# Taking arithmetic off GpSimd in a fused attention and two-stage MoE kernel: low parts by VectorE, or by a negated cast on ScalarE and an adding transfer

## The chip, the cores and the metric

One core of a Trainium2 chip runs the whole kernel. Its engines are TensorE (PE in the profile, with its weight loads shown apart as PEld), VectorE (DVE), ScalarE (ACT), GpSimd (POOL) and SyncE (SP). Each works through its own instruction list in order and waits at semaphores. Transfers (DMAs) are issued from a queue of SyncE or of GpSimd and run beside the engines. The metric is the device time of one launch in microseconds, the median over several runs.

## The reference

The input is 2 x 4096 tokens of 192 features, seen as 8192 tokens. A causal window of 7 tokens is mixed with softmax weights (8 heads of 24 features), then two wide layers follow:

```python
w = softmax(weight_gen)                       # over the 7 taps
out[b, s, h] = sum_k w[b, s, h, k] * x_pad[b, s + k, h]
gate = 1 / (1 + exp(-(x @ w_gate)))           # 192 -> 1536
x = (gate * (x @ w_val)) @ w_out              # 1536 -> 192
h = x @ w_in                                  # 192 -> 2048
P = a0 + a1*h + a2*h**2 + a3*h**3
Q = 1 + abs(b0)*abs(h) + abs(b1)*h**2
out = (P / (Q + 1e-6)) @ w_out2               # 2048 -> 192
```

The weights arrive as 64-bit floats, and everything is computed to fp32 accuracy. TensorE's fp32r format holds fewer bits, so each operand of the first three products is split into a high part (the value rounded to fp32r) and a low part (the value minus its high part), and a product is made of several matmuls.

## The kernel before, in words

The tokens are cut into 17 blocks: 15 of 4 x 128 tokens and 2 of 2 x 128. A block passes through a chain of small steps. Each step is a Python function whose name begins with `do_`; it issues a few instructions and puts the next step into a waiting list with `then(...)`. The string `ORDER` (3947 words, one for each step) says which step is issued next. This fixes the instruction order on every engine, since each engine works in the order of issue. There is no other scheduler.

The steps that matter here:

- Weight preparation: `K` loads a piece of the weights (SyncE's queue), `Ka` takes magnitudes (ACT), `Kd` packs 64-bit words into fp32 (DVE; function `pack`, lines 187 to 193), `Kh` casts the high part (ACT), and `kl` makes the low part by subtracting (POOL, line 373). `Kc` places the tails (transfers of SyncE). There are 25 pieces, 17 of which have low parts, with two subtractions each.
- Attention: `B` multiplies a shifted window by its weights (DVE, line 283). The seven products are summed by `J` (an adding transfer from GpSimd's queue, line 430) or by `j` (an addition on DVE, line 428). `Z` and `T1` transpose the block on PE; `C1` and `L1` split it into high and low.
- First layer, a unit of 128 of the 1536 columns at a time (192 units in all): `g` and `v` are five matmuls each into PSUM (`in_proj`), `S` is the sigmoid (ACT, line 490), `M` multiplies by the value (DVE, line 502), `G` casts the high part `gh` (ACT, line 508). Then `L` (on DVE) or `l` (on POOL) makes the low part `gl = g1 - gh` (line 514), and `O` is five matmuls into the accumulator.
- Second layer, 256 units: `H` is five matmuls, `A` three activations (ACT), `V` and `W` the polynomial (DVE, lines 605 and 610). Then, on pairs of units, `Q` adds the parts of the denominator by an adding transfer from GpSimd's queue (line 621), or `q` does so on DVE (line 619). `R` and `U` are activations (lines 626 and 631) that give a first reciprocal, `T` (DVE, line 614) or `t` (POOL, lines 643 and 644) together with `Y` and `D` (both DVE, line 614) finish the quotient, and `P` is the matmuls of the output product (line 669).
- `F` copies the finished block out of PSUM (ACT, line 678) and stores it.

A step with two names, such as `do_L_l`, has one body and two engines: the first name passes VectorE as `eng`, the second GpSimd. In `do_J_j` and `do_Q_q` it is the other way about: `J` and `Q` issue the transfer from GpSimd's queue, `j` and `q` add on DVE.

Buffers are rings. `bufs` tells how many tiles a name has; a tile is used again once all readers of its former content are done. PSUM has one bank each for `g` and `v`, two for `h`, and two accumulators.

Of the kernel before, what the change touches and what calls it, by code (L numbers as in the profile page):

```python
# [45 lines left out]
G v E S O E1 J l M E2 O Kd kl C2 B G g j Ka L2 Ka v Kd G H l S g M O Kd K Kc J Ka B S v g j Ka l K G O A V Z S W T1 M
C1 G kl l v X g Ka kl L1 H O A M S Kd G v l H g S O V Kc W M A v Q Kd g K R S B V Kd l G W B H M B L H O v A g Kd U O
M Q S V W G Kc L v G A Y Na M g S H O A g V W l O V T v S G R M g G W U S J H J L H v M O l D G O v M g A v S B t E l
V M G g S O A W g E1 V v Q S Q j l W H P P R Y G U A H B L R O T M v Y D U M O V g G S W A P L G H v V W P M g Ka l Kd
H S A E2 g j V v B W S A Q O V g M W G R U T Q D H L O v C2 Y H P L2 R G M P S A J v U O t A D V g l W Q H B V W O S Y  # L50
J A X P M g G H v G Y P V l S W A D M L O Z T H V g v G A W V O P S Nb W M D T1 Q Nc R v P R l M C1 B L1 P H G g H U v
A B V W l U j S Y H A A O V W g Q P T B H V W G S M g O D T Y l v R B H P O A S M G E g D Q G L P V v S E1 O g J A U l
B P R M W Q T Y G V H W U v O R M A v E2 L D V W H G L A O P Y O S H V M t Q g U G W F L v H A P V S W g T H M A S J D
P Y V J q P R A U R v W T C2 H P V M W A D O V g W H G L2 l Q B S A Y v H O U G M l g P A V P S D R V P W W T B H U T
J A V j W g v Y O H P G S M A l H v V Z X G D g M Q O A l V S W v g G W R M T1 q O U Y v P C1 l G R S D P Y O L1 H H T
A M g V A B W l G P V Q H L S P W B U g Y D A Q V S R J v W U H A R O T M H Y V W O A G v M P g U H V W D Na T S H P E
B Y g l G Q J v P A S V A E1 W g M S O v L G T Q R H P D U F L R g E2 O B A O P V W M v H D V W M S G A H g L v T Y S
P D G g V P W U C2 A l T Nb Y V H W L2 B P A M D J Q H O v M S V g Q W A O G L v S H J O V R M P G A B P J W V H U Q B
L W v G R g U A S Y T L O H V M P Y A v R D O j Nc P G g M W H V S G g W A L Z v V U O W M S Q R G v L Y P T T1 X C1 P
M L1 T O D H g v S H B A P V B W g l B A G H U S V O l M v g O Y D M A Q V S j P W R T P H Q E v G j B P U W R g A l  # L60
E1 M G O V H v D j P S B l Y A M B g G P U W T l S T D H A O G V v g W M H E2 Y J C2 Q S L A v g V M F O O W S V Q W H
R G G H B P A V U g L O A W l P L2 v H S V W D T M P g Y H q R v A G A M U D V O P P W Y V l R H G W S O v T H Q U g A
V X A D W M P J S G H J v g S V q Z L O W Na M A T G V l W R g P H P O H A Y D V W L U v Q A R V P M v W S T1 O P C1 Y
T L1 D g G H U S A M H G g A v S T L Q O V Y W B l D V W R O M E H B P A V q E1 W U G Y R v H g E2 M T R P P j U S H l
v A g G Y V W P O H A M V D C2 v W L S G T g U A M O B Q H S L Y P O V R W B A P G v H Nb V J W g T F M D l J S A B V
H D O Q g v P A S M G U G V v P L2 l g Q W H R M B W U A H l O R O G T V Y T W P L U A V P Q v Y S H M D J A g J O v S
g R W V Y M H B S A W P H Q T v V W P g H G D A S G A L D J Q P V W U P H g R V A W M X L v O Y P Nc M Z G R V U S W v
l T1 T C1 P Y O G L1 O M B H B j A l B U V H g D S O Q v G g A l S M O P R g U W Y v V G T E W H M v P H A L S E1 V W
D H T O g D M G A G V Y W P S g Q A T v S l D g l J R Q P U M H A V W V E2 R Y P B H v T U O A P M O V W B G W F H D l
S v Y C2 G M A Q H J g L2 V S O R A l W v G P P U T H M B O V J W D g S v Y H G g A A P Q B T V W S P H L R g V J P q  # L70
l W U A H M V D R O U v S A Y T T W O P Y V W P G Q H A g M V D S v R l G H O M W v H L P G U O g A A L M D V V J W v
Z X S W T1 B C1 G L1 P P Q H R H Na g A L P M O A O S T Y U B Q v V G l g Nb J D W S M V T H v M W O A B G g B v V E S
Q E1 G R l U M H P Y A R E2 O W V D P W H l A Q V Y g v H T S M U G O P W g G l T S A Y H D C2 Nc v M R l J O V W A G
g S P O P Q H j A l v g V B F S W H M V v W M G P L2 U P l A O Y g V R D P S W B T H D v J O J A H M g G U v V W A V Y
L W Q H S Q R g S U M P O H g T v B D A V A G Q T P W P G Y V L H W S P R A M j L H R P A U V W D V v H A O Z M O G g
q G V T W v W l Y T1 C1 L P S P L1 H g M U H S D A g A T O X B v G V Y S W R O U Q M g V G W B H R U v P J D T Y A P S
l V W H O l M A T V H A G v g S M P q B Q P J g W E E1 D v V l Y M R H O W U A P O H P D G l R S A F V W g G B T H V Y
A v S W U M H P Q E2 V D J L A V B v O W B C2 O G P q l M g W R P S H L2 Y G l H v g T M v D A O U V S A G M j g L S W
v P Y T H P V O g R D q P W A U H R O G M Y V S A B W v V L g U J H W H Q M S J T D g G A A O V G W V P H Y S X T W Q
v R L P A P U V Z M W O G l v T1 Na Y O M C1 L1 P R H H g v l T U B A S D O G V P g A Q W B D M l V H S W g G A Y S V  # L80
W v P T l H O J q R A E V R g H D M A P P V W q P U W G R T H H l v S Y M g v A S P B V A M g E1 O F U G E2 W J D U S
Y T l D v B H O g A O M V W v V C2 Nb H W P G H G q S L A g T Y P l M V R J L2 W A O v B P H B P G V W H U M O D J Q T
S A P A V G W L l g V H Q R v A S W Y M U Q B O H D v Nc g S P M G O V T g A Y S X G V W v j P W L H R U M A Y P H v l
D A V O R O J W M q V g W G T Z v P T1 R S l U O M C1 P G L1 D H A L g H S V A W Q v g T G V O S U H Y W R A M l O v g
E Y T E1 G M H q V D P P B S v G B l M O U W J P g v A R l V Y S H O E2 M g B A D U V Q v W T G P S W H C2 g J l A G O
V M S W H A P Q g R B v L2 G S L Y l P O T F M H D g A U v V D P G P W S H Y V W M j H g R v P A B A V T Q W L M V W U
O G O J R G B H S L P A Y U H v g D J l A V W O M Q B T S P H G j V A v W O V Y P D Q M H R W A V T D g G l P R H P U
v L W A V W S Y M T H O g Q A S P Z V v X W T1 D G C1 P P M L1 H g Na U O P B H B A S L Y Q V R v U W g J A R G T S D
H O M v T P l B g J G A V Q O W H L V Y E U B P M G v E1 S W O T A L g H M V S W D v O A G H L q M P V g R v Y R W U T
D O H P S M A A G V W V L g Y G v S H O E2 J B W F U l j C2 M A L2 P g V S H g A v Q G P B D S Q W H R V W H M O A A G  # L90
l g V B W V l v W H P M Y P S O Nb T U D Y v R T H A V g W A V Q P D G W P M U O H P G R A Y L X T H l J V S W Nc v M
A O g P S D H O j G Z V v W A l U M Q V g W G v T S q O T1 P R C1 U L1 M P H R Y T U l g v O D S g M H A V G G W B S Y
Q H A B P g S j v B l V g M A L D V W v O S G g H Y P E l R E1 M T v A P O M U G Q R W V W S Y D H A P H J B V U W v O
g H G l S P E2 B T O A V g W Y M A P Q v l S T C2 F V G D R W D H Q J P A H U M A l R V O T W v M g B O U Y P Y V L2 W
J S H v G L G g S J A B T P g H M S X V j W P Q R A O D U g v Z H L V G W P D M Q T P A H V O A L v P W O G V W Y H M
# [666 lines left out]
```

## Time and profile before

| what | value |
|---|---|
| median of 3 runs | 1437.95 us (1434.44 to 1438.52) |
| the profiled execution's own time | 1437.92 us |
| its span, first to last instruction | 1436.1 us |
| PE busy | 1337.7 us, 93% |
| DVE busy | 1313.3 us, 91% |
| ACT busy | 1176.3 us, 82% |
| POOL busy | 422.0 us, 29% |
| chain that ended last | PE 50%, DVE 25%, ACT 11%, issue 7%, DMA 4% |
| transfers from GpSimd's queue | 85.67 MB, 32.4% of the 16 DMA engines' span |
| mean granted TensorE clock | 0.993 |

"Busy" is the time in which at least one instruction of the engine runs. DVE and ACT start an instruction shortly before the one in front has ended, so the sum of single durations is a little larger than busy time. The chain is followed back from the last instruction, at each step to what released it. POOL's busy time holds its arithmetic and the issuing of its transfers.

### The profile page before, as it was taken

The numbers are of one execution on the slowest core, as the hardware profiler recorded it, in microseconds if no ns is written. First come the engines' busy times: TensorE is split into PE (matmuls) and PEld (weight loads), VectorE is DVE, ScalarE is ACT, GpSimd is POOL, SyncE is SP. The second block draws the span as 40 slices with busy tenths as digits, with TensorE's granted clock in tenths as the row PEclk, the third lists the DMA queues.
The fourth block names the chain that finished last, engine by engine and source line by source line (L and its number), as shares of the span: only waits on it lengthen the run. The fifth ranks groups of instructions, "written<-read, shape, count | busy, mean of one in ns | idle before, by whom it ended". The sixth has DMA issues, their size and how long they took to land.

```text
span 1436.1 us, 18208 instructions
## 1 busy us (share of the span) xinstructions
PE 1337.7 (93%) x6602; PEld 1144.8 (80%) x6602; DVE 1313.3 (91%) x1568; ACT 1176.3 (82%) x1761; POOL 422.0 (29%) x368
## 2 busy tenths in 40 slices
PE   1778999999999999999999999999999999989987
PEld 0556787888878788888888888888888888878886
DVE  7999898999888999889999999899999999999997
ACT  4555878989878898889988898888978889878985
POOL 3654442322132122323212222222123231452220
PEclk9999999999999999999999999999999999999999
DMA  9765343434434245444514324354425342313433
GB/s 247 185 171 132 74 97 67 85 84 99 103 68 98 45 90 107 97 107 81 120 29 85 89 59 94 67 126 78 97 41 103 78 76 68 71 32 74 85 74 67
DMA packets 48946, 130.94 MB, mean 91 GB/s; under 512 B 6236, under 2 KB 15834, under 8 KB 48856
## 3 DMA queue, kind: packets, MB, share of 16 engines
q0 software_dynamic: 27504, 85.67, 32.4%
q1 hardware_dynamic: 21064, 44.11, 10.1%
q8 instruction: 52, 0.85, 0.2%
q14 instruction: 38, 0.31, 0.1%
q10 hardware_dynamic: 288, 0.00, 0.0%
HBM read 31.51 MB, written 6.29 MB: 26 GB/s over the span
## 4 chain that ended last, share of the span: by engine, by line
PE 50%; DVE 25%; ACT 11%; issue 7%; DMA 4%; POOL 1%; SPq 1%; DVEq 0%; ACTq 0%; POOLq 0%
PE acc L669 12%; DVE v L614 6%; DVE v L605 3%; DVE v L610 3%; PE h L295 3%; DVE g L502 3%; PE h L296 2%; PE h L299 2%; PE h L297 2%; PE h L298 2%; DVE q L614 2%; DVE pr L283 2%; PE pv L295 2%; ACT v L596 2%; ACT r L598 2%
## 5 line engine op out<-in xcount | busy, mean ns | idle before, releaser
L669 PE MATMUL acc<-wo,v 128*128 128x192 f32 x2048 | 367.6, 326 | 5.8 <-DVE v L614 5.8
L669 PEld LDWEIGHTS acc<-wo,v 128*128 128x128 f32 x2048 | 340.7, 189 | 21.5 <-DVE v L614 7.1
L514 POOL TENSOR_TENSOR gl<-g,gh 128x512 fp32r<-128x512 f32 x119 | 185.2, 1559 | 428.7 <-ACT gh L508 395.3
L605 DVE TENSOR_TENSOR v<-v,h 128x512 f32<-128x512 f32 x256 | 174.3, 681 | 67.6 <-ACT r L598 66.8
L596 ACT ACTIVATE v<-h,co 128x512 f32<-128x512 f32 x256 | 176.5, 689 | 69.6 <-PE h L299 61.7
L621 POOL DMA_DIRECT2D q<-r x105 | 94.3, 898 | 408.0 <-ACT r L598 371.2
L610 DVE SCALAR_TENSOR_TENSOR v<-v,co,h 128x512 f32<-128x512 f32 x256 | 189.7, 743 | 3.8
L614 DVE SCALAR_TENSOR_TENSOR v<-v,co,r 128x1024 f32<-128x1024 f32 x128 | 185.9, 1453 | 0.4 <-ACT r L631 0.3
L614 DVE SCALAR_TENSOR_TENSOR v<-q,v 128x1024 f32<-128x1024 f32 x128 | 169.8, 1327 | 0.6
L598 ACT ACTIVATE r<-h 128x512 f32<-128x512 f32 x256 | 155.6, 608 | 8.5 <-DVE q L614 5.4
L490 ACT ACTIVATE sg<-pg 128x512 f32<-128x512 f32 x192 | 116.0, 604 | 55.6 <-PE pg L299 48.9
L614 DVE SCALAR_TENSOR_TENSOR q<-q,r 128x1024 f32<-128x1024 f32 x120 | 159.0, 1328 | 0.4 <-ACT r L631 0.4
L597 ACT ACTIVATE q<-h 128x512 f32<-128x512 f32 x256 | 153.4, 599 | 5.7 <-DVE v L614 5.7
L626 ACT ACTIVATE r<-q,co 128x1024 f32<-128x1024 f32 x128 | 147.7, 1155 | 10.4 <-DMA q<-r 5.3
L502 DVE TENSOR_TENSOR g<-sg,pv 128x512 f32<-128x512 f32 x192 | 130.6, 680 | 24.0 <-PE pv L299 18.4
L295 PE MATMUL h<-X2h,W0h 128*128 128x512 f32 (+1 forms) x272 | 118.0, 434 | 23.5 <-DVE v L610 20.2
L508 ACT CAST gh<-g 128x512 fp32r<-128x512 f32 x192 | 119.5, 629 | 23.1 <-DVE g L502 16.2
L631 ACT ACTIVATE r<-r 128x1024 f32<-128x1024 f32 x128 | 137.0, 1070 | 1.0
L296 PE MATMUL h<-X2l,W0h 128*128 128x512 f32 (+1 forms) x272 | 103.3, 380 | 0.0
L297 PE MATMUL h<-X2h,W0l 128*128 128x512 f32 (+1 forms) x272 | 103.1, 379 | 0.0
L298 PE MATMUL h<-X2h,WT 128*128 128x512 f32 (+1 forms) x272 | 103.0, 379 | 0.0
L299 PE MATMUL h<-X2l,WT 128*128 128x512 f32 (+1 forms) x272 | 102.9, 378 | 0.0
(139 smaller groups left out, 2938.5 us busy)
## 6 DMA issues: line engine op xcount, KB each, us to landing
q<-r POOLq DMA_DIRECT2D x105, 512.0 KB, 4.6
x<-pr POOLq DMA_DIRECT2D x61, 384.0 KB, 4.6
x<-in_x_dram SPq DMA_DIRECT2D x13, 960.0 KB, 5.1
out_dram<-o SPq DMA_DIRECT2D x15, 384.0 KB, 2.4
v<-in_moe_w_out_dram SPq DMA_DIRECT2D x14, 384.0 KB, 3.9
r<-r SPq DMA_DIRECT2D x28, 128.0 KB, 3.0
r<-r POOLq DMA_DIRECT2D x14, 256.0 KB, 3.6
x<-in_x_dram SPq DMA_DIRECT2D x3, 768.0 KB, 4.8
```

The lines of the kernel that those rows point to most:

```text
L295: mm(d, W0h[:, w], h[:, 0, :], start=True, stop=False)
L502: nc.vector.tensor_mul(g1, now["sg"].popleft(), pv)
L514: eng.tensor_sub(gl, g1, gh.bitcast(F32))
L596: nc.scalar.activation(v[:, e, :], ph, AF.Identity, scale=reg["a3"], bias=a2)
L597: nc.scalar.activation(q[:, e, :], ph, AF.Square, scale=reg["b1r"])
L598: nc.scalar.activation(a[:, e, :], ph, AF.Abs, scale=reg["b0"])
L605: nc.vector.tensor_mul(v, v, ph)
L610: nc.vector.scalar_tensor_tensor(out=v, in0=v, scalar=a1, in1=ph, op0=ALU.add, op1=ALU.mult)
L614: nc.vector.scalar_tensor_tensor(out=out, in0=in0, scalar=scalar, in1=in1, op0=op0, op1=op1, reverse0=neg)
L626: nc.scalar.activation(r, q, AF.Abs_reciprocal_sqrt, scale=USC, bias=usb)
L631: nc.scalar.activation(r, r, AF.Square, scale=2.0 ** -20)
L669: mm(acc[:, s // 2, (s % 2) * D:(s % 2 + 1) * D], g[:, (e * jb + s) * P:(e * jb + s + 1) * P], wo2[:, c, :], start=(c == 0 and s % 2 == 0) ...
```

## The change

GpSimd is left with issuing transfers, and with a few fills at the start.

- `do_L_l`: the form `l` no longer subtracts on GpSimd. ScalarE writes the negated value, rounded to fp32r, into `gl`, and a transfer from GpSimd's queue adds `g1` to it. `L` is as it was.
- `do_M` multiplies in place: `g1` is now the tile that the sigmoid wrote. The ring `g1` (2 tiles) is gone, `sg` has 4 tiles instead of 2, `gh` and `gl` have 3 instead of 2.
- `do_F`: the output tile has no buffer of its own and takes a tile of the ring `pr` (2 tiles), which the attention products and `Z` use too.
- `ORDER` is new throughout. It holds the same number of steps; these words are used a different number of times:

| word | what it does | before | after |
|---|---|---|---|
| `Kl` / `kl` | low parts of a weight piece on DVE / on POOL | 0 / 17 | 17 / 0 |
| `L` / `l` | gate's low part on DVE / on POOL (after: ACT and a transfer) | 73 / 119 | 135 / 57 |
| `T` / `t` | quotient step on DVE / on POOL | 120 / 8 | 128 / 0 |
| `J` / `j` | attention sum by a transfer / on DVE | 72 / 30 | 82 / 20 |
| `Q` / `q` | denominator sum by a transfer / on DVE | 105 / 23 | 113 / 15 |

The activation function's table changes whenever `S`, `R` or `Nb` (the softmax exponential) follows another of these in `ORDER`: 151 times before, counting the one at `root`, and 153 times after.

```diff
 ORDER = """
-K Na Nb Na Nc K root B K B B B Ka Ka K B K J B Nb Kd B K Kd Kh Ka Ka Kd Kh J kl Kc Kd Ka J j J Kh K K X j Z Kd kl Kh
-Nc T1 kl C1 Ka L1 K Kc g Kd v Kh S Na Kh M B B Ka B j G Kd kl g Kc B Nb v kl S K K g Kh l Ka M G kl O Kc v S Kd J Ka g
...
+Na Nb Nc K K Na root B B Ka B Ka J K B B B B J j J Kd Kh K J Ka K Kd Kl Ka K Kd Nb Kc Kd Kh Kh j Nc Z Ka X T1 C1 Kh Kd
+Kh Kl K L1 Ka g Kl v S Kc Kd B g Kh K Kl K M B G B Kc v Kl Ka S M l Kd K G J l Kl g Ka S Kd K Ka J v M g Kc Kh S K Kh
...
 """
-    bufs = dict(X2h=2, X2l=2, v=5, q=4, r=4, pr=2, sg=2, g1=2, gh=2, gl=2, wn=2, red=2, h=2)
+    bufs = dict(X2h=2, X2l=2, v=5, q=4, r=4, pr=2, sg=4, gh=3, gl=3, wn=2, red=2, h=2)
...
     def do_M(b, c, pv):
-        g1 = tl(gp, "g1", [P, T])
-        nc.vector.tensor_mul(g1, now["sg"].popleft(), pv)
+        g1 = now["sg"].popleft()
+        nc.vector.tensor_mul(g1, g1, pv)
         then("G", b, c, g1)
...
     def do_L_l(b, c, g1, gh, eng):
         gl = tl(gp, "gl", [P, T], F32R)
-        eng.tensor_sub(gl, g1, gh.bitcast(F32))
+        if eng is nc.gpsimd:
+            nc.scalar.activation(gl, g1, AF.Identity, scale=-1.0)
+            eng.dma_start(out=gl.bitcast(F32), in_=g1, accum_op=ALU.add)
+        else:
+            eng.tensor_sub(gl, g1, gh.bitcast(F32))
         then("O", b, c, gh, gl)
...
     def do_F(b, acc):
         j0, jb = BLOCKS[b]
-        o = tl(att, "o", [P, JB, D])
+        o = tl(att, "pr", [P, JB * NH, GRP]).rearrange("p n g -> p (n g)").rearrange("p (j d) -> p j d", d=D)
```

## Rows read from the trace of the kernel before

**Rows 1.** Windows, whole core: stretch, its length, busy us (instructions) of each engine.

```profile
0.00:250.00 250.00, 194.37 (x832) 155.52 (x833) 222.37 (x308) 161.55 (x278) 115.17 (x103) 0.97 0.59 139
250.00:1250.00 1000.00, 980.69 (x4758) 838.86 (x4757) 921.71 (x1080) 868.66 (x1264) 256.92 (x228) 1.00 0.41 84
1250.00:1436.10 186.10, 162.66 (x1016) 150.42 (x1014) 169.24 (x182) 146.06 (x222) 49.92 (x38) 0.98 0.33 67
```

**Rows 2.** Waits of PE: engine, line, releaser: us in total, times, longest.

```profile
PE h L459 <- DVE x L428: 29.7, 2, 29.1
PE pv L295 <- DVE g L502: 25.1, 23, 3.1
PE h L295 <- DVE v L610: 20.2, 26, 2.2
```

**Rows 3.** Windows of line 614 alone on DVE: quiet stretch, head, middle, tail.

```profile
354.80:391.40 36.60, 10.83 (x9) 1.00 0.57 118
0.00:250.00 250.00, 30.45 (x22) 0.97 0.59 139
250.00:1250.00 1000.00, 382.64 (x286) 1.00 0.41 84
1250.00:1436.10 186.10, 96.29 (x68) 0.98 0.33 67
```

**Rows 4.** Windows of line 283 on DVE: quiet stretch, head.

```profile
354.80:391.40 36.60, 2.85 (x3) 1.00 0.57 118
0.00:250.00 250.00, 36.40 (x33) 0.97 0.59 139
```

**Rows 5.** Windows of line 428 on DVE (head), then of line 619 (tail).

```profile
0.00:250.00 250.00, 11.94 (x8) 0.97 0.59 139
...
1250.00:1436.10 186.10, 5.88 (x3) 0.98 0.33 67
```

**Rows 6.** Windows of line 514 on DVE: quiet stretch, middle.

```profile
354.80:391.40 36.60, 3.42 (x5) 1.00 0.57 118
250.00:1250.00 1000.00, 48.36 (x61) 1.00 0.41 84
```

**Rows 7.** Windows of line 187 on DVE: quiet stretch, head; then of line 190.

```profile
140.80:147.60 6.80, 0.71 (x2) 1.00 0.27 83
0.00:250.00 250.00, 26.33 (x36) 0.97 0.59 139
...
140.80:147.60 6.80, 1.12 (x2) 1.00 0.27 83
0.00:250.00 250.00, 24.76 (x36) 0.97 0.59 139
```

**Rows 8.** Timelines of DVE and of POOL near 1290 us: start, us, instruction.

```profile
1285.32 1.27 DVE L614 SCALAR_TENSOR_TENSOR v<-v,co,r 128x1024 f32<-128x1024 f32 x1
1290.88 3.43 DVE L614 SCALAR_TENSOR_TENSOR v<-v,co,r 128x1024 f32<-128x1024 f32 x1
...
1290.86 2.37 POOL L644 TENSOR_TENSOR q<-q,r 128x1024 f32<-128x1024 f32 x1
```

**Rows 9.** Groups of POOL in the quiet stretch, 354.8 to 391.4 us.

```profile
L621 POOL DMA_DIRECT2D q<-r x4 | 3.7, 936 | 12.6 <-ACT r L598 12.6
```

**Rows 10.** Groups by form: DVE in the tail; ACT over the whole span.

```profile
L316 DVE TENSOR_TENSOR X2l<-h,X2h 128x256 fp32r<-128x256 f32 x2 | 0.8, 412 | 0.0
...
L508 ACT CAST gh<-g 128x512 fp32r<-128x512 f32 x192 | 119.5, 629 | 23.1 <-DVE g L502 16.2 <-PE acc L529 6.2
L490 ACT ACT_TABLE_LOAD x73 | 93.7, 1283 | 8.2 <-PE pg L299 5.9 <-DVE g L502 1.0
```

**Rows 11.** DMA issues: KB each, median us to landing; longest wait of POOL's queue.

```profile
out_dram<-o SPq DMA_DIRECT2D x15, 384.0 KB, 2.4
r<-r POOLq DMA_DIRECT2D x14, 256.0 KB, 3.6
...
POOL q L621 <- ACT r L598: 371.2, 73, 13.0
```

More of the change, by code (lines that the diff above doesn't have):

```diff
@@ L46 @@
[L46 to L95, printed above, removed]
@@ new lines @@
+L X S v J A g J O G L Z V Ka Ka W l S T1 M C1 G v Ka Kd O L1 Kd M K H H A G g l V v O S Kl Kc A g W H M S B G L g Kd V
+v A W V S Q O R L O H U B W Kc B A g M V Q Kd R v H O S M G A Y v W g L G Ka Q U M L T V O S v M H E g W A E1 J v J D
+S M Y H V A g Q v G V S W O T B l P E2 R W M H P J G U g L H B A V O A R W v J D Y V P C2 O W S H G l H Kd T M g A G S
+P V U W Q g L2 D A H v S G R V L O W O A Na M B Q T V L P H v U Y D J W Y A V P g R S P G M H O A U g v G W S H Nb B L
+P T V W J g D S M A v Nc V H M Z Q L A V W g S Q R v O G P W Y U T1 M X l v T M P C1 L1 O G H l R A D H A P T g V W B
@@ new lines @@
+B q S H G V v W A O J V W O Y R M D g G Q H S P v U L B M A g S H A V L v W g Y V T W M G O O D U S P P L R T G J E H
+Q L E1 G L Y E2 g R v M H O v S g O A A V W U V S q B M P W D g T G U Y Y C2 J H P S O F A V v L2 H B W A D P P V H Q
+G M R g W v L T H B O A G M A P V W R U J D U H S Q V W P L P H T j g l A B A S V W G V v R M Q X Y W P H O H U v D A
+g O P R S Y Y T j P G V M L v W g A H M l V W v S G T D U A O Z M V g W v P T1 O G S L T C1 L1 P Q H l H Na R M Y g v
+D P G A V U W S A B H O g Q O G D P V M A S G Q W T L B H B P g v V R l U A W V W R J M Y D l H S A V W O v M H Y T g
@@ new lines @@
+P G S H A O V A B g S v L W P Q g D U R G M V P W J E E1 Q L F H R v O M H S v T Y A V g W O D U H G S A j B M P U P
+E2 L Y B G v Nb O O T L Q A V W P M G V R J P B g C2 L D H A O V G W v S Y W O l H T g P A Q M S H v U g D A S P V W T
+V H g W L2 M J H J Y R A U V D v M P G A Q W Nc v S P G H O A T Q Z L M P V V W g v W S T1 P R Y C1 G M D L O L1 O H U
+L g G v A X Q B V H L W P B R S Y H g A V M O O U v G A T L V W O H Y S g M R v W S E G g P S U B T D M E1 g L A H q v
+P V G j J A W L O H T D S R E2 B P g Q U O Y G A R V M S v T G W P M L D H V W G L U Y v M O A g P Y H G S L J A v B g
@@ new lines @@
+Q M V V F S W W C2 v R O L2 J H A D H B U V P W P A H A M Y Q l V P g W V O P R T S W U H v D B A T J V Y G q G H A W
+g M J X P O S T L D P H g V R Z A G W v H Q S M L V O W g U A L V v H P M S D T P R P W G O v U A V Q W T1 Y D G R O
+C1 l U L1 T P H A g P B Q V W L B M H H T O S A V g W Y D G O v P B M L A H S R v U A Q O Y M g R S V v G W H J E D Y
+P A M l g U V P P W G T S H B V g W E1 Y T Q E2 v Na G l H A V S M g L W R U J O P D G H A D A O V O C2 V W F v W H q
+P S g A Y L2 H Q P S M J R V v T W P D A H L O V M U G A L W V v W R M H B Y g T P B J Nb v P S H A g V G D S j M P U
@@ new lines @@
+g G W A O v H Q T L S V W A R G B H M v O X Nc L P V U O g P M Q W L H A J G Y R L D v P V S W G A O M T V Q g W v Z
+T1 G S Y O D C1 L1 P L l g H B U S M H g A S v A G V T Q g M W Y S R v B H V O D J L R A M P V W g U U W P O T H Y G O
+S B A L H D g E G V W Q Y A Q E1 v S P V R H W U g M T P D v M A H R U A J O V L G P W G P Y T V H F O q A W L B P T R
+V H v E2 L S A P U D O W M g B H V Y S v A P M g S G V v W H M L g Q J C2 A W v V M G S O g L2 G P H L Q W J v R B Y H
+T O D M S A A G L V V P W O Q B g O P U W T J H D Y v H X R U P Y M A J S v V W A P T H V G D G g Z M Q L W A P V S L
@@ new lines @@
+l g A S V Y P W j V g Q R D W U H O P A M G B l V T W H R v U j A D M H P O V S Y v W g H M O P G G D Z v A A V Y V W
+W Q P H L R T S O M g A U S v V Q W T1 C1 L O P G M L1 D L H R g H G Y A v S T M V Q U P W O G D L G R P L g H v T A P
+O V X W O S A U B E B M Y V L g W S H A V v T g H G Q E1 A S P P W M Q D v V R W B g Y J U H H A J L V Y S A E2 P P G
+B O M v W g F V W M H S T v H D O A V M C2 W L L2 G g P S A q J L B D v R P H U G V O M W q G B A g H R U V O P W P A
+T J Y R V H D S G L J v Q P W O H l Y U g T A M Na S v V W G g l A Y V P W S H H R D O T g A L U M Q V R S B v A G P M
@@ new lines @@
+H G M T v S A g V J B D L W P G A Q P M E2 S H L V v R W g F M v A V D R W J U Z P Y T1 U C1 P L1 S H A H Q T Y V A W
+V W O G C2 O G T H A g L2 P P M S R D V L H W A O L U H Q V R W g A H D T G Y Q P P U V W P S H A g v L P D Y V W A V
+T W H P S R H A D V Q M U W A R P Y H T V W A O V U Q v G H W D A Q M O R V G T W U H Y T l Y P P H O A A R Q V D W P
+P g H V E W U S E1 H D v A V A g W E2 V Y W S L R P C2 T L2 U P D H F O A M H T V A W P V P Q R Y W D G H U Q A V v H
+M A P W V T P W H v Q R U Y H A g G l P V A M W R H T S V W D P O H Y A V U Q A D P W T P V Q H Y W R A U D v V G P H
@@ L110 @@
+l M P A W T H R Q A U O G l V Y W l P H A Q P V D W H P Y V A W T V O H R U D W A O R U Y V T W O Y Q P E H A V H E1 W
+A P P V E2 C2 T L2 R F W H D H U D T A V A Q V W P P H R Y W P U H D A Q V A R T P W V H Y W P A Q V U D H W A V T P H
+R P W U A Q H Y Y P A F R Q D T V P P D U T R Y U P V D W W T P Y P P D P P F
 """
```

46 lines of the change are left out of this document (29 added, 17 removed).

## The prediction, made before the changed kernel was run

> **What bounds the kernel now.** I first split the span into a head (0 to 250 us, in which the weights are prepared), a middle and a tail (from 1250 us, in which the gate units run out) and read each engine's busy time there [rows 1]. In the middle TensorE is busy 980.7 of 1000 us; nothing that leaves its matmuls alone can win more than the missing 19.3 us. In the head it is busy 194.4 of 250, so 55.6 us are missing; in the tail 162.7 of 186.1, so 23.4. DVE is the other full engine: 222.4 of 250, 921.7 of 1000, 169.2 of 186.1. ScalarE has 88, 131 and 40 us to spare.
>
> Then I read whom TensorE waits for [rows 2]. One wait of 29.1 us is the start, until the first attention block is summed. The other large ones name DVE: the value matmuls wait for the product `M` that empties their bank (25.1 us in 23 waits, 1.09 us each), the `H` matmuls for `W`, line 610, for the same reason (20.2 us in 26 waits, 0.78 each). TensorE loses time because DVE reads PSUM late, by about a microsecond at a time.
>
> Why is DVE late? The timelines show two executions of the same instruction [rows 8]. At 1285.32 us line 614 takes 1.27 us. At 1290.88 us it takes 3.43: GpSimd had begun its line 644 at 1290.86, which runs 2.37 us, and 2.37 + 1.27 is 3.64, close to it. The DVE instruction, whose two inputs both lie in SBUF, behaves as if it stood still while GpSimd's arithmetic ran. So I looked for a stretch in which GpSimd only issues transfers, 354.8 to 391.4 us [rows 9], and compared the same lines there and elsewhere.
>
> **The change part by part.** *What goes away.* In the quiet stretch line 614 takes 10.83/9 = 1.203 us [rows 3]. At that price its 22, 286 and 68 instructions in head, middle and tail would take 26.5, 344.1 and 81.8 us; they take 30.45, 382.64 and 96.29, so 4.0, 38.5 and 14.5 us too much. In the same way:
>
> - line 283: 0.95 quiet, 33 in the head, 36.40 - 31.35 = 5.0 too much [rows 4];
> - line 428, the same shape with two inputs, 11.94 - 8 x 0.95 = 4.3 in the head; line 619, of the shape of 614, 5.88 - 3 x 1.203 = 2.3 in the tail [rows 5];
> - line 514: 0.684 quiet, 48.36 - 61 x 0.684 = 6.6 in the middle [rows 6];
> - the weight packing, lines 187 and 190: 0.355 and 0.56 quiet, 36 of each in the head, so 26.33 - 12.8 = 13.5 and 24.76 - 20.2 = 4.6 [rows 7] (shapes differ, but 384 columns is near their mean).
>
> That is 31.4 us in the head, 45.1 in the middle, 16.8 in the tail, a lower bound since small groups are left out. With no arithmetic on GpSimd all of it should go. That transfers' issue doesn't do the same is borne out by the quiet stretch itself, which holds four issues of line 621 alone at 0.94 us each [rows 9].
>
> *What DVE gets.* Counts are from the order strings. 62 more `L` at 0.684 [rows 6]: +42.4. The 34 subtractions of the 17 `Kl`: nine of 512 columns at 0.684, 17 of 256 at 0.412 [rows 10], eight of 128 at an estimated 0.27 (the step from 512 to 256, halved again): +15.4. Eight `T` more, line 614 at 1.203: +9.6. Ten `j` fewer at 0.95, eight `q` fewer at 1.203: -9.5 and -9.6. The sum over the run is +48.3 against at least 93.3 taken off.
>
> By place: up to the 37th `O` before, and the 23rd `H` after, which stand at the same amount of matmul work, the new order has given DVE all of `Kl` (+15.4), five `L` (+3.4), three `T` (+3.6), one `q` (+1.2), five `j` fewer (-4.8), one `B` fewer (-0.95), and one `M`, one `V` and two `W` more, taken at 0.68 each (+2.7): +20.6. The head's net is 31.4 - 20.6 = 10.8 us off DVE. From word 3487 on, where both orders stand at their 205th `P`: four `L` and four `T` more, three `q` and one `Y` fewer, the rest about even: 2.7 + 4.8 - 3.6 - 1.2 = +2.7. The tail's net is 16.8 - 2.7 = 14.1 us off. The middle gets the remaining 25, against 45.1: 20 us off 921.7.
>
> *What ScalarE gets.* 57 negated casts at the price of the cast of line 508, 0.629, so +35.9, and two table loads more at 1.283 [rows 10], +2.6; together 38.5; by the place of the 57 `l` in the order some 14 of the casts' 35.9 fall in the head, where it is free for 88 us, and 18 in the middle, where it is free for 131 [rows 1]. Costed at nothing; if that cover were gone they would cost at most these 38.5.
>
> *The new way of a low part.* Before, GpSimd subtracted as soon as `gh` was there. Now: cast 0.63, issue 0.94 [rows 9], landing 3.6 for a transfer of this size from this queue [rows 11], 5.2 us from `l` to `O`. Between an `l` and its `O` the new order puts 3 matmul steps at the least, 5 at the tenth percentile and 7 in the median (before: 0, 0 and 3). A step of five matmuls is 980.69/4758 x 5 = 1.03 us by [rows 1], and a `P` has eight, so 5 steps cover the path and nearly all units are covered. After each of these issues GpSimd's queue holds the transfers of `Q` and `J`, for which `R` and `Z` wait. The longest wait in that queue was 13.0 us before [rows 11]; its engine keeps 70% of its time free. I take nothing, with an upper bound below.
>
> *Rings.* In-place `M` keeps an `sg` tile until the low part is made, and there are four instead of two plus two. At nothing. `F` now takes a `pr` tile that a `B` needs again: the store lands in 2.4 us [rows 11], and by the order the next user comes at least five matmul steps later. At nothing; were all 15 large stores uncovered, it would be 36 us on DVE.
>
> *The sum.* Head: 11 us of DVE's load, where DVE is 89% busy and TensorE waits for it. (Loads and casts could hold it instead: 0 to 26.5, the missing 55.6 less the first wait.) Middle: TensorE's 19.3 us are mostly waits of about 1 us on DVE, and the one held instruction that I looked at came 2.2 us late; of the two ends, none and all, I take 14, nearer to all, since DVE's spare time rises from 78 to about 98 us. Tail: 14. Together 39: the span 1436.1 becomes 1397.1, and with the 1.8 us that lie around the span in the profiled execution (1437.92) that is 1399 us. That execution's time is the median's to 0.03 us.
>
> **The rivals.** *Late low parts* (slower). The place is `O` behind `l`, 57 times. For: the path grows from one subtraction to 5.2 us in three stations, and one queue orders everything. Against: the order's distance. If each came late by the 1.09 us that one wait on DVE costs now [rows 2], 57 x 1.09 = 62 us come on top: 1461. It decides from 39/57 = 0.7 us each.
>
> *DVE isn't relieved* (the change doesn't do what it says). If issuing held DVE as arithmetic did, DVE would carry its 48.3 us more with nothing off: head +20.6, tail +2.7, and the middle at 947 of 1000, say 10 more, so 1438 + 33 = 1471. Against: [rows 9] beside the quiet prices.
>
> *The head is held by loads and casts, and the middle's waits stay.* Then only the tail's 14 us come: 1424. For: ScalarE's chain lies between the two DVE steps of a weight piece, and each `Kl` must now wait in DVE's list for its `Kh`.
>
> *The hold the other way round.* In the head, line 187 has a single tensor input and was still held by GpSimd's arithmetic (26.33 against 12.8 us) [rows 7]. If such an instruction in turn held up an issue, each of the 36 would delay transfers by its 0.355 us, at most 12.8 us in the head: 1399 + 11, the head's gain, = 1410. The Trainium skill, "SBUF — State Buffer", section "SBUF: two separate sides", says that GpSimd can't write a transfer's descriptors while DVE runs an operation on two ports, and this speaks against moving more sums to GpSimd's queue. By that rule it would be 1410, by the rows 1399; no run here shows an issue so held, and past the head no line 187 is left.
>
> **How the numbers follow.** Chances: the forecast 0.68, with its own range 1374 to 1414; the hold the other way round 0.04; loads and casts 0.11; `pr` stores partly uncovered, about 1425, 0.03; late low parts 0.10; no relief 0.04. The low end is what remains when nearly all missing TensorE time but the first wait goes: 26.5 + 19.3 + 23.4 = 69.2 gives 1369, and I stop at 1374. The high end takes in the tail-only case and the stores: 1432. Left out are the two slow rivals and a sliver below. About 0.3%, 4 us, is what a measurement of this kernel can tell from no change. Faster by more than that: 0.68 + 0.04 + 0.11, and 0.02 of the stores, less 0.03 for a forecast that several small costs eat up: 0.82. Slower: 0.10 + 0.04, less 0.02 for late parts that just cancel the gain: 0.12. The rest, 0.06, is no change.
>
> **What would show it.** Right: line 614 at 1.20 to 1.24 us, 283 at 0.95 and 187 near 0.35 throughout; DVE busy at about 1260 to 1270 although it holds more instructions; TensorE's waits on `M` and line 610 at half or less; the head to the same matmul work some 11 us shorter. Wrong: `O`'s matmuls waiting for a transfer into `gl`; GpSimd's issues, or ScalarE's casts of `gh`, queued for long behind one wait; `B` or `F` waiting for a store; DVE instructions still stretched. If DVE is relieved as said and the time stays, then the head hung on loads and the middle on TensorE alone.

## The result, and the profile after

The changed kernel takes 1397.25 us (median of 4 runs, 1395.94 to 1397.84), beside 1437.93 us for the kernel before on the same chip: ratio 0.9721, 95% interval 0.9704 to 0.9738. The profiled execution took 1397.84 us, with a span of 1396.0. Line numbers after the change are up to 4 higher than before: line 614 before is line 618 now, 610 is 614, 514 is 518, 621 is 625.

The page of the changed kernel, its busy times, its GpSimd queue and its chain:

```profile
PE 1330.1 (95%) x6602; PEld 1150.1 (82%) x6602; DVE 1241.8 (89%) x1654; ACT 1203.7 (86%) x1820; POOL 233.8 (17%) x274
...
q0 software_dynamic: 38304, 108.54, 42.7%
...
PE 49%; DVE 5%; ACT 5%; issue 3%; DMA 2%; POOL 0%; POOLq 0%; ACTq 0%; DVEq 0%
```

DVE runs 86 instructions more than before (1654 against 1568) and is busy 71.5 us less. Its share of the chain that ended last fell from 25% to 5%; the shares named add up to 97% of the span before and to 64% now, so the two chains compare only roughly. GpSimd's queue moves a quarter more bytes.

For the stages I cut the new span where TensorE has done the same number of matmuls as at the cuts of [rows 1]. The windows of the changed kernel, with the columns of [rows 1]:

```profile
0.00:244.00 244.00, 195.43 (x832) 157.98 (x833) 197.41 (x345) 173.46 (x300) 51.28 (x64) 0.96 0.78 174
244.00:1223.10 979.10, 973.97 (x4752) 841.27 (x4751) 889.20 (x1124) 882.29 (x1296) 155.74 (x180) 1.00 0.49 98
1223.10:1396.00 172.90, 160.70 (x1021) 150.84 (x1019) 155.15 (x187) 147.96 (x226) 26.77 (x31) 0.98 0.46 91
```

The head is 6.0 us shorter, the middle 20.9, the tail 13.2: together 40.1 of span. The second cut lies five matmuls early; cut at exactly the same matmuls, the stages are 5.9, 20.1 and 14.1 shorter. The forecast was 11, 14 and 14.

TensorE's waits in the changed kernel:

```profile
PE h L459 <- DVE x L428: 30.1, 1, 30.1
PE pg L298 <- DMA WT<-r: 8.7, 4, 3.8
PE acc L673 <- DVE v L618: 3.2, 2, 2.0
PE pv L295 <- DVE sg L502: 3.0, 6, 0.8
PE h L295 <- DVE v L614: 2.8, 6, 0.6
...
PE acc L534 <- DMA gl<-sg: 1.7, 2, 1.4
```

The two large waits on DVE of [rows 2], 25.1 and 20.2 us, are 3.0 and 2.8. A new one stands second: matmuls that wait for a transfer into `WT`, the weight tails, and all 8.7 us of it lie in the head. Low parts that come late by the new way cost 1.7 us.

DVE's groups by form in the changed kernel, then line 187 alone in the first 250 us, then line 618 alone over the whole run:

```profile
L618 DVE SCALAR_TENSOR_TENSOR v<-v,co,r 128x1024 f32<-128x1024 f32 x128 | 163.3, 1278 | 1.1 <-ACT r L635 1.1
L618 DVE SCALAR_TENSOR_TENSOR q<-q,r 128x1024 f32<-128x1024 f32 x128 | 155.9, 1218 | 0.1
L518 DVE TENSOR_TENSOR gl<-sg,gh 128x512 fp32r<-128x512 f32 x135 | 91.9, 684 | 1.2 <-ACT gh L508 1.2
L283 DVE TENSOR_TENSOR pr<-x,wn 128x768 f32<-128x768 f32 x86 | 81.6, 951 | 2.1 <-DMA x<-pr 2.0
...
```

```profile
0.00:250.00 250.00, 11.46 (x36) 0.96 0.77 171
```

```profile
0.00:1396.00 1396.00, 470.08 (x384) 0.99 0.53 110
```

The means are over the whole run, and those of `L` (0.684) and `B` (0.951) are the quiet prices of [rows 4, 6]. Line 618 comes to 470.08/384 = 1.224 us, a little above the 1.203 of [rows 3]. Line 187 fell from 26.33 to 11.46 us [rows 7].

What the new low part costs, from the changed kernel's groups of ACT and POOL and its list of transfers:

```profile
L515 ACT ACTIVATE gl<-sg 128x512 fp32r<-128x512 f32 x57 | 36.3, 640 | 0.0
```

```profile
L516 POOL DMA_DIRECT2D gl<-sg x57 | 51.5, 909 | 233.4 <-ACT gl L515 161.0 <-DVE OT L373 18.5 <-DVE v L609 17.3
```

```profile
x<-pr POOLq DMA_DIRECT2D x70, 384.0 KB, 5.6
gl<-sg POOLq DMA_DIRECT2D x57, 256.0 KB, 3.8
...
out_dram<-pr SPq DMA_DIRECT2D x15, 384.0 KB, 3.1
```

Cast 0.640, issue 0.909 and landing 3.8 us stand against 0.629, 0.94 and 3.6 in the forecast.

**The head.** The same stretch, 50 to 150 us, first in the kernel before, then in the changed one:

```profile
50.00:150.00 100.00, 84.34 (x338) 64.54 (x338) 94.69 (x126) 55.21 (x107) 52.90 (x48) 0.94 0.60 152
```

```profile
50.00:150.00 100.00, 85.61 (x341) 66.89 (x340) 72.16 (x138) 61.22 (x121) 23.82 (x27) 0.91 0.90 208
```

DVE went from 94.7% to 72.2% busy, and yet only three matmuls more were done. The DMA engines went from 60% to 90% of their time, and TensorE's granted clock from 0.94 to 0.91. TensorE's timeline in the changed kernel shows how the two belong together (start, us, instruction):

```profile
51.03 0.39 PE L297 MATMUL pg<-X1h,W0l 128*128 128x512 f32 x1
54.17 0.47 PE L298 MATMUL pg<-X1h,WT 128*128 128x512 f32 x1 [2.74 <-DMA WT<-r]
...
55.44 0.63 PE L533 MATMUL acc<-gh,OT 128*128 128x512 f32 x1
55.87 0.63 PE L534 MATMUL acc<-gl,O0h 128*128 128x512 f32 x1
...
58.58 0.39 PE L295 MATMUL pg<-X1h,W0h 128*128 128x512 f32 x1
58.81 0.39 PE L296 MATMUL pg<-X1l,W0h 128*128 128x512 f32 x1
```

A matmul waits 2.74 us for `WT`. Matmuls then start 0.43 us apart instead of 0.23 until about 58 us. The granted clock of 56 to 60 us is 0.72, a mean of the two levels of 1.2 and 2.4 GHz. TensorE had waited 2.74 us just before the clock fell, and with the wait came some eight matmuls that took 0.2 us longer each.

### The profile page after: what moved, and what is told of

It reads as the page before. It is cut to its first block, busy times and chain, and to the rows that moved or that the text cites. A ratio compares the mean times of both kernels' runs of the same rounds, so it can differ in the third digit from the quotient of the medians.

```text
span 1396.0 us, 18221 instructions
## 1 busy us (share of the span) xinstructions
PE 1330.1 (95%) x6602; PEld 1150.1 (82%) x6602; DVE 1241.8 (89%) x1654; ACT 1203.7 (86%) x1820; POOL 233.8 (17%) x274
## 4 chain that ended last, share of the span: by engine, by line
PE 49%; DVE 5%; ACT 5%; issue 3%; DMA 2%; POOL 0%; POOLq 0%; ACTq 0%; DVEq 0%
PE acc L673 13%; PE h L295 3%; PE h L296 2%; PE h L297 2%; PE h L298 2%; PE h L299 2%; PE pv L295 2%; PE pg L296 2%; PE pg L295 2%; PE pg L297 2%; PE pg L298 2%; PE pg L299 2%; PE pv L296 2%; PE pv L297 2%; PE acc L533 2%
## 5 line engine op out<-in xcount | busy, mean ns | idle before, releaser
L625 POOL DMA_DIRECT2D q<-r x113 | 104.0, 921 | 604.2 <-ACT r L602 527.1
L618 DVE SCALAR_TENSOR_TENSOR v<-v,co,r 128x1024 f32<-128x1024 f32 x128 | 163.3, 1278 | 1.1 <-ACT r L635 1.1
L618 DVE SCALAR_TENSOR_TENSOR v<-q,v 128x1024 f32<-128x1024 f32 x128 | 155.8, 1219 | 0.4
L618 DVE SCALAR_TENSOR_TENSOR q<-q,r 128x1024 f32<-128x1024 f32 x128 | 155.9, 1218 | 0.1
L502 DVE TENSOR_TENSOR sg<-sg,pv 128x512 f32<-128x512 f32 x192 | 130.8, 681 | 26.8 <-PE pv L299 16.4
L508 ACT CAST gh<-sg 128x512 fp32r<-128x512 f32 x192 | 119.4, 626 | 11.1 <-DVE sg L502 9.9
L430 POOL DMA_DIRECT2D x<-pr x78 | 79.2, 1016 | 264.7 <-DVE pr L283 110.3
```

What stands on the lines that cost most here:

```text
L618: nc.vector.scalar_tensor_tensor(out=out, in0=in0, scalar=scalar, in1=in1, op0=op0, op1=op1, reverse0=neg)
```

## The experiments

Ratios are to the kernel before, on the same chip, with 95% intervals; windows and rows are of one profiled execution each. Where a run changes `ORDER`, only words are swapped and everything else stays, unless said.

**1. The old order, with no arithmetic on GpSimd** (`old_order_dve`). The kernel before, with every `kl`, `t` and `l` of its order on DVE:

```diff
 ORDER = """
-... J kl Kc Kd Ka J j J Kh K K X j Z Kd kl Kh Nc T1 kl C1 ... g Kh l Ka M G kl O ...
+... J Kl Kc Kd Ka J j J Kh K K X j Z Kd Kl Kh Nc T1 Kl C1 ... g Kh L Ka M G Kl O ...
```

> The kernel before with its own order and rings, but every low part and every quotient step on VectorE (all 119 l, the 17 pairs of kl and the 8 t): GpSimd does no arithmetic and nothing is replaced by a transfer. Theory 1 (GpSimd's arithmetic held DVE's two-input instructions, and that was dear): DVE loses the 93 us or more of holds and gains 119 x 0.684 + 15.4 + 9.6 = 106 us, so it is as full as before, 1310 to 1330 us busy, and the time is near the kernel before, 1430 to 1455. Theory 2 (there was no such cost, the new order made the gain): DVE would be busy 1420 and the time well over 1480.

Measured: 1423.89 us, ratio 0.9909 (0.9892 to 0.9927). Its busy times and two of its DVE groups:

```profile
PE 1338.9 (94%) x6602; PEld 1147.5 (81%) x6602; DVE 1291.2 (91%) x1729; ACT 1177.1 (83%) x1761; POOL 167.6 (12%) x199
```

```profile
L613 DVE SCALAR_TENSOR_TENSOR q<-q,r 128x1024 f32<-128x1024 f32 x128 | 155.7, 1219 | 1.2 <-ACT r L630 1.2
L513 DVE TENSOR_TENSOR gl<-g,gh 128x512 fp32r<-128x512 f32 x192 | 131.1, 685 | 6.8 <-ACT gh L507 6.8
```

DVE does 161 instructions more than before (119 `l`, 34 in `kl`, 8 `t`), which at their prices is 119 x 0.685 + 15.4 + 8 x 1.219, about 107 us, and is still busy 22 us less than the 1313.3 of before. That would make the holds 129 us, but it sets single durations, which overlap a little, beside busy time. The durations of the same forms of instruction in the two traces differ by 113 us in all, 49 of them on line 614, 15 on line 187 and 13 on line 283; that is the size of the holds. The forecast's 93.3 was a lower bound and holds as one; this run's expectation reckoned with little more than that and missed both ranges, 1310 to 1330 us busy and 1430 to 1455 in all. About 13 of the 40 us come from this alone (1436.7 to 1423.9 on this chip).

**2. The old order with the new bodies** (`old_order`). The changed kernel with the order of before (`kl` and `t` on DVE, all 119 `l` by cast and transfer), two tiles each for `gh` and `gl`, and a buffer of its own for `F`:

```diff
-    bufs = dict(X2h=2, X2l=2, v=5, q=4, r=4, pr=2, sg=4, gh=3, gl=3, wn=2, red=2, h=2)
+    bufs = dict(X2h=2, X2l=2, v=5, q=4, r=4, pr=2, sg=4, gh=2, gl=2, wn=2, red=2, h=2)
...
-        o = tl(att, "pr", [P, JB * NH, GRP]).rearrange("p n g -> p (n g)").rearrange("p (j d) -> p j d", d=D)
+        o = tl(att, "o", [P, JB, D])
```

> The old order with the new bodies: kl and t on VectorE, all 119 l as a negated cast and an adding transfer, sg with 4 tiles, gh and gl with 2, the output tile in its own buffer. DVE has no holds and only 25 us more than before less the 93, so about 1235 busy. Theory 1 alone would give 1400 to 1420. The rival that the path of a low part is too long for its place (median 3 matmul steps from l to O in the old order against a path of 5.2 us) expects the matmuls of O to wait for transfers into gl and a time above the kernel before, 1450 or more.

Measured: 1607.1 us, ratio 1.1197 (1.1171 to 1.1224). TensorE's waits there:

```profile
PE acc L533 <- DMA gl<-sg: 142.7, 56, 7.2
```

DVE is relieved even further (1229.2 us busy), and the kernel is 12% slower: 56 low parts are late, by 2.5 us each on average. This is the forecast's slower rival. In the changed kernel only 1.7 us are lost so, and its order puts more matmuls between `l` and `O`, which is the forecast's reason. The smaller rings may have a part in it; they weren't separated from the order.

**3 and 4. What holds DVE: reads or writes by GpSimd** (`pool_reads`, `pool_writes`). The changed kernel, with useless work on GpSimd behind 112 of the `gh` casts: three subtractions of 64 columns, or eight fills of 64 columns.

```diff
         nc.scalar.copy(gh, g1)
+        if b > 1 and c % 12 in (0, 1, 3, 4, 6, 7, 9, 10):
+            for k in range(3):
+                nc.gpsimd.tensor_sub(scratch, W0h[:, 64 * k:64 * k + 64].bitcast(F32), W0l[:, 64 * k:64 * k + 64].bitcast(F32))
```

The other run has `for k in range(8): nc.gpsimd.memset(scratch, 0.0)` in that place.

> The changed kernel, with useless arithmetic put back on GpSimd behind 112 casts of gh from block 2 on: three subtractions of 64 columns that read two SBUF operands each. Nobody waits for them. Theory 1: two-input DVE instructions stretch again (line 618 above its 1.22 to 1.28 us), DVE busy goes up by 20 to 60 us, and the time by 8 to 25 us. Theory 2 (the order made the gain): within 4 us of the changed kernel.

> The same places as in the run with added subtractions, but eight fills of 64 columns each, which write SBUF and read nothing. If reading is what holds DVE, the two-input instructions keep their 0.684 and 1.22 us and the time stays within 4 us of the changed kernel. If any work on GpSimd holds DVE, or if a busier GpSimd queue delays the transfers, it is slower by 8 us or more.

Measured: 1398.92 us (0.9731, 0.9715 to 0.9748) with the subtractions, 1396.11 (0.9722, 0.9704 to 0.9739) with the fills. For each, its added group on POOL and one DVE group, `pool_reads` first:

```profile
L513 POOL TENSOR_TENSOR scratch<-W0h,W0l 128x64 f32<-128x64 f32 x336 | 240.6, 716 | 18.9
```

```profile
L623 DVE SCALAR_TENSOR_TENSOR q<-q,r 128x1024 f32<-128x1024 f32 x128 | 158.6, 1239 | 0.0
```

```profile
L513 POOL MEMSET scratch<- 128x64 f32 x896 | 174.3, 195 | 45.9
```

```profile
L623 DVE SCALAR_TENSOR_TENSOR q<-q,r 128x1024 f32<-128x1024 f32 x128 | 156.0, 1219 | 0.1
```

Fills leave DVE as it is (1219 ns, busy 1242.1 us against 1241.8). Subtractions stretch it (1239 ns, busy 1253.5). So by these two runs it is arithmetic that reads tiles which holds DVE; the forecast had named GpSimd's arithmetic, without parting reads from writes. But 240.6 us of GpSimd's time held only 11.7 us of DVE's, and the time moved by less than 2 us, where 8 to 25 were expected: the dose was too small to show in the time. The Trainium skill, "SBUF — State Buffer", section "Who interferes with whom", says that a DVE instruction with two SBUF inputs contends with a GpSimd instruction that reads SBUF and not with one that only writes it; these two runs agree.

**5 and 6. The 57 low parts made in other ways, in the new order** (`l_on_pool`, `l_all_dve`). In the first, GpSimd subtracts them again; in the second, every `l` of the order is an `L`.

```diff
         if eng is nc.gpsimd:
-            nc.scalar.activation(gl, g1, AF.Identity, scale=-1.0)
-            eng.dma_start(out=gl.bitcast(F32), in_=g1, accum_op=ALU.add)
+            eng.tensor_sub(gl, g1, gh.bitcast(F32))
```

```diff
-Kh Kl K L1 Ka g Kl v S Kc Kd B g Kh K Kl K M B G B Kc v Kl Ka S M l Kd K G J l Kl g Ka S Kd ...
+Kh Kl K L1 Ka g Kl v S Kc Kd B g Kh K Kl K M B G B Kc v Kl Ka S M L Kd K G J L Kl g Ka S Kd ...
```

> The changed kernel and its order, but the 57 l are subtractions on GpSimd again, as before the change. ScalarE is freed of 57 casts (36 us), 57 transfers vanish, and DVE's two-input instructions meet 57 GpSimd subtractions of 512 columns. Before, some 100 such subtractions in middle and tail made about 60 us of holds, so 57 should give DVE 25 to 35 us more busy time (1268 to 1277). Theory 1 (holds cost time where TensorE and DVE are both nearly full): slower than the changed kernel by 4 to 15 us. The rival (TensorE sets the pace alone once the order leaves room): within 3 us, or faster where the shorter path of a low part helps.

> The changed kernel and its order, but all 57 l are subtractions on VectorE: no holds, no casts, no adding transfers of low parts. DVE gets 57 x 0.684 = 39 us more, 1281 busy of about 1400, ScalarE 36 us less. If DVE's spare time is what the 57 transfers buy, TensorE's waits on DVE come back and it is slower than the changed kernel by 5 to 20 us; if TensorE alone sets the pace, within 3 us.

Measured: 1401.73 us (0.9756, 0.974 to 0.9773) on GpSimd, 1394.81 (0.9707, 0.9691 to 0.9723) on DVE. The busy times, first of `l_on_pool`, then of `l_all_dve`, whose windows follow:

```profile
PE 1326.8 (95%) x6602; PEld 1144.6 (82%) x6602; DVE 1284.1 (92%) x1654; ACT 1174.9 (84%) x1763; POOL 266.2 (19%) x274
```

```profile
PE 1325.0 (95%) x6602; PEld 1142.2 (82%) x6602; DVE 1273.9 (91%) x1711; ACT 1176.4 (84%) x1763; POOL 183.5 (13%) x217
```

```profile
0.00:231.70 231.70, 189.79 (x832) 151.96 (x833) 210.36 (x368) 162.16 (x278) 31.96 (x42) 0.99 0.68 158
231.70:1220.60 988.90, 976.05 (x4753) 840.96 (x4752) 906.45 (x1153) 870.83 (x1270) 130.87 (x151) 1.00 0.44 89
...
```

By these two executions DVE is busier when GpSimd makes the 57 subtractions (1284.1 us) than when DVE makes them itself (1273.9). Each takes (1284.1 - 1241.8) / 57 = 0.74 us of DVE's time in holds; made on DVE, each adds (1273.9 - 1241.8) / 57 = 0.56 by the same measure. The second reading is that the transfers don't pay over the run: with plain subtractions on DVE the kernel is no slower than the changed one (2.4 us faster by the medians, with intervals that overlap). By the windows the transfers win 9.8 us in the middle (979.1 against 988.9) and lose 12.3 in the head (244.0 against 231.7).

**7. Subtractions on DVE in the head alone** (`head_l_dve`). The changed kernel with its first 22 `l`, all that fall in the head, as `L`; the swap is that of run 6, ended there.

> The changed kernel with only its first 22 l (those in the head, to 244 us) on VectorE. In the changed kernel DVE is idle for 28 of the 100 us from 50 to 150, while the DMA engines are 90% busy and matmuls wait for transfers into WT. If the head now hangs on transfers, 22 fewer of 256 KB shorten the waits for WT and the head by 2 to 6 us: 1391 to 1395. If it hangs on DVE after all, 15 us more on DVE make it slower, 1400 to 1410.

Measured: 1389.25 us, ratio 0.9677 (0.9656 to 0.9697), better than expected: 8.0 us under the changed kernel by the medians (the profiled execution was the fastest of four, 1385.79). Its windows by stage, then 50 to 150 us:

```profile
0.00:231.10 231.10, 188.95 (x833) 151.39 (x834) 209.95 (x368) 162.18 (x279) 31.66 (x42) 1.00 0.68 158
231.10:1210.80 979.70, 974.01 (x4752) 841.74 (x4751) 889.04 (x1122) 881.02 (x1295) 155.32 (x179) 1.00 0.49 98
...
```

```profile
50.00:150.00 100.00, 92.54 (x400) 71.90 (x399) 94.32 (x174) 66.69 (x124) 11.24 (x13) 1.00 0.68 169
```

DVE has 12.5 us more to do in the head, and the head is 12.9 us shorter. In the 100 us shown, 400 matmuls are done instead of 341, at a granted clock of 1.00. TensorE's idle time in the head fell by 6.4 us (48.6 to 42.2), its busy time for one matmul more by 6.5 us, at a granted clock of 1.00 instead of 0.96: about half of the gain lies in matmuls that took less time, at the higher clock.

**8. Is it the traffic?** (`head_traffic`). Run 7, with a useless transfer of 192 KB from GpSimd's queue behind each of the 22 `L`, into output rows that are written again later:

```diff
             eng.tensor_sub(gl, g1, gh.bitcast(F32))
+            if made["gl"] in early:
+                j = TJ - 2 - 2 * early.index(made["gl"])
+                nc.gpsimd.dma_start(out=ov[:, j:j + 2, :].rearrange("p j d -> p (j d)"), in_=g1[:, 0:2 * D])
```

> The run with the first 22 low parts on VectorE, plus a useless transfer behind each of these 22, from GpSimd's queue: 192 KB of the gate tile into rows of the output that are stored over later. Nobody waits for them, but a tile of sg stays taken until its transfer has landed. If the 13 us that the head lost to the 22 adding transfers were their load on the DMA engines and queue, a good part comes back: matmuls wait for WT again and the head's matmul work is reached at 236 to 244 us instead of 231; 1393 to 1400 in all. If the loss was the longer path from gh to O, nothing changes: 1387 to 1391.

Measured: 1395.5 us, ratio 0.9708 (0.9693 to 0.9723). Its head, then 50 to 150 us:

```profile
0.00:237.40 237.40, 193.47 (x832) 156.00 (x833) 210.03 (x368) 162.59 (x278) 44.69 (x64) 0.97 0.71 172
```

```profile
50.00:150.00 100.00, 91.08 (x380) 71.52 (x379) 88.52 (x166) 62.18 (x115) 18.40 (x26) 0.96 0.73 196
```

Nothing waits for these 22 transfers, and they give back 6.3 us: half of the 12.9 by the heads' windows, three quarters of the 8.0 by the medians. So transfers that nobody waits for bring back half of the head's loss or more; whether by their load on queue and engines or by the `sg` tile that each keeps until it has landed, this run can't tell. The rest can lie in the larger size of the adding transfers (256 KB), in the adding, or in the way `l` to `O` itself; that wasn't separated. The waits for `WT` didn't come back in this run, so that particular wait isn't the only form the loss can take.

**9 to 12. The first wait.** TensorE's first transposes start at 30.1 us. DVE waits for the last of four adding transfers of the first block, as its timeline in the changed kernel shows:

```profile
29.02 0.96 DVE L428 TENSOR_TENSOR x<-x,X2h 128x768 f32<-128x768 f32 x1 [5.24 <-DMA x<-X2h]
```

In `first_j` one of these sums is made on DVE; `head_l_first_j` is this and run 7 together; in `head_l_first_all_j` all six sums of the block are on DVE; in `early_start` they also stand earlier in the order, and the steps that follow them too.

```diff
-... J K B B B B J j J Kd Kh K J Ka K Kd Kl Ka K Kd Nb Kc Kd Kh Kh j Nc Z ...
+... J K B B B B J j J Kd Kh K Ka K Kd Kl Ka K Kd Nb Kc Kd Kh Kh j j Nc Z ...
```

```diff
-... j K B B B B j j j Kd Kh K Ka K Kd Kl Ka K Kd Nb Kc Kd Kh Kh j j Nc Z Ka X T1 C1 Kh Kd ...
+... j K B B B B j j j Kd Kh K j j Z T1 Kl Kc C1 L1 Ka K Kd Ka K g Kd Nb X Kd Kh Kh v S Nc ...
```

The first diff is `first_j` against the changed kernel, the second `early_start` against `head_l_first_all_j`.

> The changed kernel with one sum of the first block added on DVE in place of the adding transfer that landed last (6.6 us from issue to landing, DVE waiting for it 5.2 us). The first transposes start at 30.1 us in the changed kernel; they should start at 25 to 26. If the start sets the rest, 3 to 5 us faster (1392 to 1394); if the weights' arrival sets the next stretch, the gain is gone by the 100th microsecond and the time is within 2 us.

> Both edits of the two runs that were faster than the changed kernel: the first 22 low parts on VectorE, and one sum of the first block on VectorE. Alone they gave 1389.3 and 1393.1 against 1397.3. If they act at different places (the first 30 us, and 40 to 150 us) they add up: 1384 to 1386. If the head's weights set the pace after the start, the second adds nothing: 1388 to 1390.

> As the run with both edits, but all six sums of the first block on VectorE, none as a transfer. DVE gets three additions more (2.6 us) before the first transposes but waits for no landing; the transposes should start at 24 to 25 us instead of 26. 1383 to 1386 if the start counts, and no better than with one sum if DVE, now full in the head, pays for the additions.

> The first 22 low parts on VectorE and all six sums of the first block on VectorE, as in the run before, but the last two sums right behind the first weight piece, with the first block's copies, transposes and splits moved up behind them and the other weight pieces after. In the run before, those sums stood behind four weight pieces and the transposes started at 29.0 us, no earlier than before. Here they should start at 21 to 23 us. If the start sets what follows, 4 to 7 us are won on the run with the low parts alone (1389.3): 1382 to 1385. If the arrival of the weights sets the pace after the start, the gain stays under 3 us, as with one sum (1386.4).

| run | time, us | ratio (95%) | first transposes, us |
|---|---|---|---|
| `first_j` | 1393.07 | 0.9696 (0.968 to 0.9712) | 26.1 |
| `head_l_first_j` | 1386.38 | 0.9649 (0.9636 to 0.9662) | 25.8 |
| `head_l_first_all_j` | 1387.72 | 0.9652 (0.9633 to 0.9671) | 29.0 |
| `early_start` | 1386.6 | 0.9662 (0.9637 to 0.9686) | 22.8 |

One sum moved wins 4.0 us of start and 4.2 of time, which the intervals alone would hardly tell from nothing; that run 7 with it is 2.9 us under run 7 points the same way. With all six on DVE the transposes start at 29.0, not the 24 or 25 expected: the last two sums stand behind four weight pieces in DVE's list, as in `head_l_first_j`, and the three further additions in front make DVE begin those pieces at 19.7 us instead of 16.4. Moved up, they start at 22.8 us, and nothing is won. TensorE's timeline in `early_start`, with its idle time and releaser at the right:

```profile
31.50 0.70 PE L294 MATMUL pg<-X1h,W0h 128*128 128x512 f32 x1 [2.50 <-ACT sg L489]
35.10 0.79 PE L296 MATMUL pg<-X1h,W0l 128*128 128x512 f32 x1 [2.48 <-DVE W0l L372]
37.87 0.79 PE L297 MATMUL pg<-X1h,WT 128*128 128x512 f32 x1 [1.97 <-DMA WT<-r]
```

The early start waits for a sigmoid and for weights that aren't ready yet. `head_l_first_j` is the best version found: 1386.38 us, 10.9 under the changed kernel; the intervals of the last three overlap.

## Why the prediction was right, and what was mis-sized

- **The holds, the main step, held.** The lines came near their quiet prices, and runs 3 to 5 put holds back by GpSimd's arithmetic alone, in runs 3 and 4 only where it reads. Line 614's share was put too high (57 us for 49, from a price of nine instructions), and the groups left out were worth more: 113 us by run 1, for 93.3. That, and 7 us more of starts that overlap in DVE's list, is why DVE fell to 1241.8 us and not to 1260 or 1270.
- **DVE's load is not the whole of it.** The forecast's sum turns load taken off DVE into time. Runs 1 and 5 have DVE about equally busy (1291.2 and 1284.1 us) and lie 22 us apart (1423.9 and 1401.7). In the head the second has 2.2 us more for DVE and is 7.9 us shorter, `old_order_dve` first:

```profile
0.00:246.40 246.40, 197.65 (x832) 158.61 (x833) 213.85 (x371) 162.00 (x278) 27.36 (x37) 0.95 0.61 142
```

```profile
0.00:238.50 238.50, 193.08 (x833) 155.42 (x834) 216.07 (x346) 162.47 (x279) 65.23 (x64) 0.97 0.67 153
```

Besides the 57 subtractions on GpSimd, what parts the two runs is the new order with its rings and bodies. No term of the sum holds it, and which part of it does it wasn't separated. So the forecast credits DVE's relief with some of what the order gives.

- **The tail** was forecast at 14 us and gave 13.2 (14.1 at the same matmuls), and DVE's load there fell by 14.1, as forecast (169.24 to 155.15). In run 1 it falls by 7.7 and the tail is 5.5 shorter.
- **The middle was mis-sized**: 20.9 us (20.1) for 14. The forecast said that nothing that leaves the matmuls alone could win more than the missing 19.3 us. TensorE's missing time did fall as forecast, from 19.3 to 5.1 us, which is 14.2. But its busy time fell too, by 6.7 us for six matmuls fewer. The missing time was no upper bound, as the timeline above shows: a matmul's row lasts 0.39 us and the next starts 0.23 after it, so the first 0.16 us of each wait count as busy. The middle has 31 waits of TensorE before and 7 now, the largest groups these, before and after:

```profile
PE h L295 <- DVE v L610: 7.0, 11, 1.3
PE pv L295 <- DVE g L502: 6.3, 11, 1.3
```

```profile
PE h L295 <- DVE v L614: 1.0, 3, 0.5
PE pv L295 <- DVE sg L502: 0.5, 2, 0.3
```

24 waits fewer at 0.16 us are an estimated 4 us of the 6.7, and six matmuls at 0.2 about 1; the rest wasn't traced.

- **The head was mis-sized**: 6.0 us for 11, by the step "Head: 11 us of DVE's load, where DVE is 89% busy and TensorE waits for it". DVE's load to the same matmul fell by 25 us, more than twice the 10.8 forecast, but DVE stopped being what holds the head: in runs 6 and 7 it has 12 to 13 us more to do there, and the head is 12 to 13 us shorter. Weight transfers came late and TensorE's clock fell. The step that failed stands under the new way of a low part, which costed the transfers by the path of one of them and by GpSimd's idle time, and took nothing; the load on the DMA engines, which rose from 60% to 90% between 50 and 150 us, was in no term. Run 7 sizes what the 22 low parts by cast and transfer cost, net of making them on DVE, at 12.9 us of the head (8.0 by the medians), and run 8 puts 6.3 of it back with plain transfers. The mis-sizings of head and middle nearly cancel: that the total came within 2 us is luck.
- **The order covers the new path**, as worked out from the distances: 1.7 us of late low parts, against 142.7 in run 2 with its old order and smaller rings. ScalarE's busy time grew by 27.4 us (38.5 forecast), at nothing.
- **The hold the other way round** wasn't seen at the size it would need. Issues in the head took 0.92 us for `gl`, and those of line 621 went from 0.90 to 1.00: 1 us in all over ten, not 12.8.
- **The large stores from `pr`** cost nothing seen: no wait of the trace names one, and `F` waits 1.9 us in all for its tile, for an adding transfer that still reads it.
- **Where the 40 us come from**: taking arithmetic off GpSimd in the old order gives 13 us (run 1); the new order, rings and bodies, with the sums it moves to transfers and plain subtractions on DVE, 29 more (1423.9 to 1394.8, run 6), not separated any further; the 57 low parts by cast and transfer add nothing to that, and perhaps give 2 us back (to 1397.2).
